# Attention and two MLPs in one kernel: the attention's pieces in a new order on TensorE, one ring for scores and transposes, and room of their own for three MLP operands

## Chip, cores and metric

One core of a Trainium2 chip. The metric is the device time of one execution in microseconds, the median of several runs. PE is TensorE, ACT ScalarE, DVE VectorE, POOL GpSimd, SP the engine that issues most DMAs.

## What is computed

Sigmoid attention over 4 batches, 12 heads, 448 positions of 64 values; its output, 1792 tokens of 768 values, goes through two MLPs of width 2048.

```python
scores = scale * np.matmul(q, k.transpose(0, 1, 3, 2)) - np.log(S)
attn = 1.0 / (1.0 + np.exp(-scores))
x = np.matmul(attn, v)                       # then (B*S, H*D)
h = x @ moe_w_in                             # first MLP: ELU
x = np.where(h > 0.0, h, np.exp(np.minimum(h, 0.0)) - 1.0) @ moe_w_out
h = x @ moe2_w_in                            # second MLP: h - tanh(h)
out = (h - np.tanh(h)) @ moe2_w_out
```

## The kernel before, in words

**Attention** runs over 24 pairs of heads (pair n is batch n // 6, heads 2(n % 6) and the next). Almost every product is made of three passes over a value's head and rest (the value rounded to fp32r, and what is left), so each operand needs a copy (the head, on ACT or DVE) and a subtraction (the rest, on DVE). For pair n:

- `t` (`transpose`, L302): four transposes of the queries (`t`, 0; 112-row pieces) and four of the keys (`t`, 1; 128-row pieces) on PE, into PSUM.
- `head` (L306, ACT) and `rest` (L311, DVE) bring them to SBUF as head and rest, in `e`, of which there are two, for even and odd pairs.
- `s` (`scores`, L336): for u = 0, 1, 2 six matmuls each, in which the two heads of the pair lie on the upper and lower 64 rows of the array (64x128 in the profile); for u = 3, the 64 positions left over of both heads together, three matmuls of 128x128.
- `sig` (L350, ACT): the sigmoid of one `s` piece. For u = 3 the result is split again: `ahead` (L359, ACT) and `arest` (L365, DVE).
- `pv` (L377, L384): for u = 0, 1, 2 two fp32 matmuls on 64 columns of the array each (128x64; four rows in the profile); for u = 3 three of 128x128. All four add into one PSUM bank.
- `xdone` (L395, ACT) copies that bank to `R0a`, `R0b`, `R1a` or `R1b`, the MLP's input (first or second half of the tokens; heads 0 to 5 or 6 to 11). POOL's `vhead` and `vrest` prepare the values for `pv`, 3.

PSUM during attention: three tiles of two banks for scores (`pss`, used in turn, (4n + u) % 3), one bank for transposes (`pst`), one for the output (`psv`).

**The order.** Each engine's instructions are written down by `Sched`: every operation has a queue, a cost, its predecessors and a rank. A greedy run over these costs starts, on each engine, what can start first, and of equal ones the lowest rank. `attention` chains its own operations: within one engine they stand strictly in the order of their rank, `when` = n x CYCLE + PHASES + SHIFTS (L70 to L84). PHASES says where in a pair's cycle a piece stands, and negative values put it into an earlier pair's. MLP operations carry ranks above 10^6 (but for the first weight loads, which have fixed ones) and fill in where the costs leave an engine free. On the chip each engine then works through its list in this order.

**The first MLP** begins right behind. It multiplies by Strassen-like schemes: the input of each half s of the tokens is turned into seven operands (B11, B21, T1, T2, B22, T3, T4; the T are differences), each with `x_sum` (L686, DVE), `x_head` (L692, ACT) and `x_rest` (L695, DVE), and the weights of each group into W0 to W3 (`w_head` L659, `w_rest` L662). Seven products P1, P2, P5, P6, P3, P7, P4 of nine matmuls each (`m_p`, L723) follow per group and half. P1, P2, P5 read B11, B21, T1 in tile `XA`, which exists from the start; P6, P3, P7, P4 read T2, B22, T3, T4 in `XB0`, which is opened (`open_late`) in the room that attention leaves, so its operands wait for the last `xdone` (`FIRST`, `before_late`). P3 and P7 read the weights W2, which are written over the inputs in `R0a` and `R0b` once all seven operands have been made from them. `snap` (L735) takes PSUM results out, `h_add` (L740), `g_a`, `g_b`, `g_c` finish them, `g_store` (L779, SP) stores them as `hidden`.

What is behind the opening (the rest of both MLPs, some 800 us) keeps its order on every engine.

Of the kernel before, what the change touches and what calls it, by code (L numbers as in the profile page):

```python
# [16 lines left out]
class Sched:  # L17
# [52 lines left out]
CYCLE = 8976  # L70
PHASES = {
    ("ahead", 0): 13136, ("ahead", 1): 14379, ("ahead", 2): 7982, ("ahead", 3): 8647,
    ("arest", 0): 13603, ("arest", 1): 17151, ("arest", 2): 17901, ("arest", 3): 18480,
    ("head", 0): -11764, ("head", 1): -8326, ("ldk",): -43986, ("ldv",): -25986, ("pv", 0): -2074,
    ("pv", 1): 1121, ("pv", 2): 3246, ("pv", 3): 4235, ("rest", 0): -564, ("rest", 1): 4498,
    ("s", 0): -12986, ("s", 1): -11085, ("s", 2): -11076, ("s", 3): -7628, ("sig", 0): 316,
    ("sig", 1): 2153, ("sig", 2): 3042, ("sig", 3): 3134, ("t", 0): -23560, ("t", 1): -17682,
    ("vhead",): 12413, ("vrest",): 13504, ("xdone",): 15024,
# [8 lines left out]
def kernel(  # L87
# [27 lines left out]
    ON_ACT = (2, 3)  # L115
    NAN, NAH, NAF, NVL, NL = 8, 3, 2, 2, 2
# [26 lines left out]
    XA = raw_p.tile([128, 3 * SLOT[0]], F32R, tag="XA", name="XA")  # L143
    raws = {(tag, 0): raw_p.tile([128, n], F32, tag=tag, name=tag) for tag, n in RAW.items()}
# [9 lines left out]
    with tc.manual_schedule():  # L154
# [7 lines left out]
        def attention():  # L162
# [178 lines left out]
            def width(u):  # L341
                return 2 if u < 3 else 1
# [1159 lines left out]
```

## Time and profile before

| | us |
|---|---|
| median of three runs | 1044.06 (1043.88 to 1046.54) |
| the profiled execution | 1043.71 |
| its span, first to last instruction | 1041.9 |
| PE busy in it | 1025.7 (98%) |
| PE weight loads | 877.8 (84%) |
| DVE busy | 635.3 (61%) |
| ACT busy | 579.1 (56%) |
| POOL busy | 93.2 (9%) |

The busy time of PE counts matmuls that overlap in the pipeline as one stretch, with modelled ends; it says that PE has work, not that it works at its densest. What a piece takes is read better from the start of its first matmul to the start of the next piece's. Attention lasts from the start to about 183 us; in each 20 us of it up to 180 us the mean granted clock is 1.00 (of 2.4 GHz).

### The profile page before, as it was taken

How to read it: one execution, taken by the hardware profiler on the slowest of the kernel's cores; microseconds unless marked ns; L12 is line 12 of the kernel's file. 1: busy time of each engine (PE TensorE's matmuls, PEld its weight loads, DVE VectorE, ACT ScalarE, POOL GpSimd, SP SyncE). 2: the span in 40 equal slices, each digit the busy share in tenths (PEclk: the TensorE clock that was granted, in tenths of full speed). 3: DMA queues.
4: the chain of work that ended last, by engine and by line, in shares of the span. 5: the costliest groups of instructions: out<-in, count | busy, mean ns of one | idle time of the engine just before them, and what ended most of it. 6: DMA issues, size and time to landing. Idle time of an engine off the chain costs nothing.

```text
span 1041.9 us, 15205 instructions
## 1 busy us (share of the span) xinstructions
PE 1025.7 (98%) x5420; PEld 877.8 (84%) x5420; DVE 635.3 (61%) x901; ACT 579.1 (56%) x930; POOL 93.2 (9%) x122
## 2 busy tenths in 40 slices
PE   8999999999999999999999999999999999999998
PEld 5555554779899998878899998889888999999998
DVE  2332354877676756665553459766666779665673
ACT  6777877866666665443332426433444546445652
POOL 1101110201221100000000202111111000000000
PEclk9999999999999999999999999999999999999999
DMA  7564430167766658999986300544444795455443
GB/s 171 156 165 122 95 75 23 36 208 239 257 227 222 225 169 289 345 324 368 357 297 207 104 1 21 212 154 154 155 154 154 266 320 198 133 170 172 130 136 92
DMA packets 151738, 190.26 MB, mean 183 GB/s; under 512 B 57072, under 2 KB 114672, under 8 KB 151408
## 3 DMA queue, kind: packets, MB, share of 16 engines
q1 hardware_dynamic: 150096, 188.72, 55.7%
q8 instruction: 42, 0.69, 0.3%
q10 hardware_dynamic: 1568, 0.59, 0.2%
q14 instruction: 32, 0.26, 0.1%
HBM read 125.30 MB, written 63.96 MB: 182 GB/s over the span
## 4 chain that ended last, share of the span: by engine, by line
PE 86%; DMA 5%; DVE 4%; ACT 2%; issue 1%; SPq 1%; ACTq 0%; DVEq 0%
PE psa L723 12%; PE psd L723 10%; PE psx L723 9%; PE sps L336 6%; PE pvps L377 6%; PE psb L723 5%; PE psa L869 3%; PE psx L869 3%; PE psb L869 3%; PE psw L869 3%; PE psv L869 3%; PE psu L869 3%; PE psd L925 3%; PE psx L925 3%; PE tps L302 2%; PE psb L925 2%
## 5 line engine op out<-in xcount | busy, mean ns | idle before, releaser
L311 DVE TENSOR_TENSOR e<-tps,e 128x448 fp32r<-128x448 f32 (+1 forms) x46 | 30.1, 654 | 91.2 <-ACT e L306 91.2
L336 PEld LDWEIGHTS sps<-e 64*128 64x128 f32 (+1 forms) x504 | 51.1, 185 | 25.7 <-ACT e L306 15.5
L336 PE MATMUL sps<-e 64*128 64x448 f32 (+1 forms) x504 | 71.3, 378 | 0.0
L377 PE MATMUL pvps<-an,vl 128*64 128x448 f32 x288 | 69.4, 563 | 0.6 <-ACT R1b L395 0.6
L350 ACT ACTIVATE an<-sps,bias 128x896 f32<-128x896 f32 x72 | 69.7, 1009 | 0.3 <-PE sps L336 0.3
L645 POOL TENSOR_TENSOR second<-second 128x384 f32<-128x384 f32 x15 | 18.0, 1199 | 509.3 <-DMA second<-kept_wi 370.1
L723 PE MATMUL psa<-XB,W 128*128 128x512 f32 x192 | 54.3, 391 | 0.4 <-ACT t L735 0.4
L850 ACT ACTIVATE XB<-t 128x384 fp32r<-128x384 f32 (+1 forms) x59 | 33.3, 566 | 18.2 <-PE psw L869 3.7
L723 PEld LDWEIGHTS psa<-XB,W 128*128 128x128 f32 x192 | 36.0, 188 | 8.4 <-ACT t L735 0.9
L645 POOL TENSOR_TENSOR first<-first,second 128x384 f32<-128x384 f32 x30 | 37.0, 1233 | 40.5 <-DVE R0b L662 39.3
L306 ACT ACTIVATE e<-tps 128x448 fp32r<-128x448 f32 (+1 forms) x46 | 26.2, 570 | 23.8 <-PE tps L302 21.3
L752 ACT ACTIVATE spare<-t 128x512 f32<-128x512 f32 (+1 forms) x30 | 17.5, 583 | 36.6 <-DVE t L740 34.1
L854 DVE TENSOR_TENSOR XB<-t,XB 128x384 fp32r<-128x384 f32 (+1 forms) x59 | 35.7, 614 | 3.3 <-ACT XB L850 3.3
L750 ACT ACTIVATE spare<-t 128x512 f32<-128x512 f32 (+1 forms) x39 | 22.4, 577 | 25.4 <-DVE t L740 23.8
L850 ACT ACTIVATE XB<-spare 128x384 fp32r<-128x384 f32 (+1 forms) x45 | 25.6, 569 | 19.4 <-DMA spare<-x_forms 9.3
L906 ACT ACTIVATE XB<-t 128x384 fp32r<-128x384 f32 (+1 forms) x36 | 20.1, 566 | 28.9 <-PE psb L925 15.1
L756 ACT ACTIVATE spare<-spare 128x384 f32<-128x384 f32 (+1 forms) x64 | 35.7, 572 | 0.7
L723 PE MATMUL psa<-XA,e 128*128 128x512 f32 x144 | 36.0, 394 | 0.0
L723 PE MATMUL psb<-XA,e 128*128 128x512 f32 x144 | 35.8, 393 | 0.0
L723 PE MATMUL psd<-XA,W 128*128 128x512 f32 x144 | 35.2, 389 | 0.0
L566 DVE TENSOR_SCALAR first<-first 128x768 int32<-128x768 int32 x32 | 17.9, 558 | 27.1 <-ACT first L563 26.8
L723 PE MATMUL psa<-XB,R0a 128*128 128x512 f32 x96 | 31.9, 416 | 2.2 <-ACT t L735 2.2
(400 smaller groups left out, 2751.1 us busy)
## 6 DMA issues: line engine op xcount, KB each, us to landing
R1b<-in_moe_w_out_dram SPq DMA_DIRECT2D x20, 768.0 KB, 5.8
first<-in_moe_w_in_dram SPq DMA_DIRECT2D x14, 768.0 KB, 6.3
second<-in_moe_w_in_dram SPq DMA_DIRECT2D x14, 768.0 KB, 6.6
x_forms<-R1b SPq DMA_DIRECT2D x29, 256.0 KB, 2.0
t<-x_forms SPq DMA_DIRECT2D x27, 256.0 KB, 3.2
hidden<-t SPq DMA_DIRECT2D x26, 256.0 KB, 2.0
R1a<-in_moe_w_out_dram SPq DMA_DIRECT2D x8, 768.0 KB, 7.7
t<-x_forms SPq DMA_DIRECT2D x32, 192.0 KB, 2.4
```

Source lines behind the costliest of these rows:

```text
L306: nc.scalar.activation(out=es[n % 2][:, slot, :W], in_=T["t", n, w][:, :W], func=ACTF.Copy)
L311: nc.vector.tensor_tensor(out=e[:, to, :W], in0=T.pop(("t", n, w))[:, :W], in1=f(e[:, slot, :W]), op=ALU.subtract)
L336: nc.tensor.matmul(out=ps[:, j, :S], lhsT=e[lanes, ks, cols], rhs=e[lanes, qs, :S], start=(x == 0), stop=(x == 2),)
L350: nc.scalar.activation(out=a[:, :m], in_=T.pop(("s", n, u))[:, :m, :S], func=ACTF.Sigmoid, bias=bias, scale=scale)
L377: nc.tensor.matmul(out=ps[D * j:D * j + D], lhsT=vl[n // NL % NVL][:, n % NL, 5 * j + u], rhs=a[:, j], start=(u == 0), stop=False,)
L645: by.tensor_tensor(out=out, in0=x, in1=y, op=op)
L723: nc.tensor.matmul(out=ps, lhsT=w[wz][:, k0:k0 + 128], rhs=xs[xz][:, kk], start=(opens and n == 0), stop=(n == 3 * KH - 1), skip_group_che ...
L756: nc.scalar.activation(out=r, in_=r, func=ACTF.Exp, scale=-1.0)
L850: nc.scalar.activation(out=at_place(og_place[s, p, j], 0, 1)[:, :HW[s]], in_=T["graw", s, p, j], func=ACTF.Copy)
L854: nc.vector.tensor_tensor(out=lo, in0=T.pop(("graw", s, p, j)), in1=f(hi), op=ALU.subtract)
L869: nc.tensor.matmul(out=T["o2", tag], lhsT=g[:, t * 128:t * 128 + 128], rhs=w[:, j % 2 * DH:(j % 2 + 1) * DH], start=(p in OPENS and j == 0 ...
L925: nc.tensor.matmul(out=ps, lhsT=lhsT, rhs=rhs, start=(opens and x == 0), stop=(ends_ and x == 2), skip_group_check=True,)
```

## The change

Attention's table of ranks is new (one cycle is 6900 instead of 8976 units, and almost all of SHIFTS goes). Its effect on the order is shown below. Besides:

- Scores and transposes share the ring of three two-bank tiles, five uses a pair, (5n + u) % 3; both transposes of a pair go into the two halves of one tile, written before its turn comes (`before_s` names what must have been read). The bank of their own goes.
- The output gets a second bank, used in turn: `pv`, 0 waits for `xdone` two pairs back, not one.
- `ahead` and `xdone` move from ACT to DVE.
- Fewer SBUF buffers for attention (`an` 8 to 6, `ah` 3 to 2); the room goes to `XB0`, now with T2, B22 and T3 alone and open from the start, so that these can be made as soon as their inputs are there. T4 goes to a small tile `XB2`, opened late as before. Places of later operands are renamed to match, in the same room.
- W1 and W3 and three PSUM banks, opened early, wait for `xdone` of the last pair but one too.

```diff
-CYCLE = 8976
+CYCLE = 6900
 PHASES = {
-    ("head", 0): -11764, ("head", 1): -8326, ("ldk",): -43986, ("ldv",): -25986, ("pv", 0): -2074,
...
+    ("s", 0): 0, ("s", 1): 620, ("s", 2): 1240, ("s", 3): 1900, ("pv", 3): CYCLE + 2500,
+    ("t", 1): 3100 - 2 * CYCLE, ("t", 0): 3500 - 2 * CYCLE, ("pv", 0): 4000, ("pv", 1): 4900, ("pv", 2): 5800,
...
+    ("ldk",): 4000 - 5 * CYCLE, ("ldv",): 3300 - 2 * CYCLE,
 }
...
-    ON_ACT = (2, 3)
-    NAN, NAH, NAF, NVL, NL = 8, 3, 2, 2, 2
+    NAN, NAH, NAF, NVL, NL = 6, 2, 2, 2, 2
...
+    XB0 = raw_p.tile([128, 3 * SLOT[0]], F32R, tag="XB0", name="XB0")
...
-            pst = apool("pst", 1, early, space=bass.MemoryType.PSUM, side="right")
...
-            psv = apool("psv", 1, space=bass.MemoryType.PSUM)
+            psv = [apool("psv0", 1, early, space=bass.MemoryType.PSUM, side="right")]
+            psv += [apool("psv1", 1, space=bass.MemoryType.PSUM)]
...
-                if (n, w) == (0, 1):
-                    ps = pss[0].tile([128, 2, BK], F32, tag="s", name="sps")[:, 0]
...
-                T["t", n, w] = ps
+                if ("tps", n) not in T:
+                    T["tps", n] = pss[(5 * n - 6) % 3].tile([128, 2, BK], F32, tag="s", name="sps")
+                T["t", n, w] = ps = T["tps", n][:, w]
...
-                T["s", n, u] = ps = pss[(4 * n + u) % 3].tile([128, 2, BK], F32, tag="s", name="sps")
+                T["s", n, u] = ps = pss[(5 * n + u) % 3].tile([128, 2, BK], F32, tag="s", name="sps")
...
-                if u in ON_ACT:
-                    nc.scalar.activation(out=t[:, 0], in_=a[:, 0], func=ACTF.Copy)
-                else:
-                    nc.vector.tensor_copy(out=t[:, 0], in_=a[:, 0])
+                nc.vector.tensor_copy(out=t[:, 0], in_=a[:, 0])
...
-                    T["o", n] = psv.tile([128, 512], F32, tag="o", name="pvps")[:, :S]
+                    T["o", n] = psv[n % 2].tile([128, 512], F32, tag="o", name="pvps")[:, :S]
...
+            def before_s(n, x):
+
+                n, x = divmod(5 * n + x - 3, 5)
+                return [("sig", n, x)] if x < 4 else [("rest", n + 2, 0), ("rest", n + 2, 1)]
...
-                op("xdone", n, (), "ACT", 700 if pairs[n][0] == 2 else 550, xdone, [("pv", n, 3)] + before)
+                op("xdone", n, (), "DVE", 700 if pairs[n][0] == 2 else 620, xdone, [("pv", n, 3)] + before)
...
-                    for n, s in enumerate(SLOT):
-                        tiles[f"XB{n}"] = pools["xb"].tile([128, 4 * s], F32R, tag=f"XB{n}", name=f"XB{n}")
+                    for name, n in (("XB1", 4 * SLOT[1]), ("XB2", SLOT[0])):
+                        tiles[name] = pools["xb"].tile([128, n], F32R, tag=name, name=name)
...
-                    name, at = ("XA", j) if j < 3 else ("XB0", j - 3)
+                    name, at = ("XA", "XB0", "XB2")[j // 3], j % 3
...
+            before_early += [("xdone", last - 1)]
...
-                     "XA": [], "XB0": before_late, "XB1": before_late, "R0a": [], "R0b": [], "R1a": [], "R1b": []}
+                     "XA": [], "XB0": [], "XB1": before_late, "XB2": before_late, "R0a": [], "R0b": [], "R1a": [], "R1b": []}
```

PE, one pair in the middle of attention, before (`sps` scores, `tps` transposes, `pvps` the output's bank; x18 are the scores of u = 0, 1, 2, x3 with `e` those of u = 3, x3 with `ah` is `pv`, 3):

```order
L336 MATMUL sps<-e_122 128x448 x18
L377 MATMUL pvps<-an,vl_119 64x448 x2
L302 MATMUL tps<-ident,first 128x128 x4
L377 MATMUL pvps<-an,vl_119 64x448 x2
L336 MATMUL sps<-e_122 128x448 x3
L377 MATMUL pvps<-an,vl_119 64x448 x2
L302 MATMUL tps<-ident,first 128x112 x4
L384 MATMUL pvps<-ah,vs_120 128x448 x3
```

and in the changed kernel (`sps` now holds scores and transposes):

```order
L333 MATMUL sps<-e_81 128x448 x21
L378 MATMUL pvps<-ah,vs_122 128x448 x3
L299 MATMUL sps<-ident,kq_118 128x128 x4
L299 MATMUL sps<-ident,kq_118 128x112 x4
L371 MATMUL pvps<-an,vl_119 64x448 x6
```

Eight pieces have become five: all scores together, the `pv`, 3 of the pair before, both transposes (of the pair after next), the other three `pv` together.

DVE, end of attention and start of the MLP, before (`XB_1909` is tile XB0, `XB_1910` XB1, `R0b<-second,R0a` the weights W2; the `e`, `W` rows are W0, W1, W3):

```order
L662 TENSOR_TENSOR e_80<-spare,e_80 128x768
L365 TENSOR_TENSOR ah<-a,ah 128x448
L662 TENSOR_TENSOR W_1868<-second,W_1868 128x768
L662 TENSOR_TENSOR W_1869<-spare,e_80 128x384
L695 TENSOR_TENSOR XB_1909<-R0b,XB_1909 128x1536
L695 TENSOR_TENSOR XB_1909<-R0a,XB_1909 128x1536 x2
L695 TENSOR_TENSOR XB_1909<-R0b,XB_1909 128x1536
L740 TENSOR_TENSOR t<-t,psb 128x512
L695 TENSOR_TENSOR XB_1910<-R1a,XB_1910 128x1152
L662 TENSOR_TENSOR R0b<-second,R0a 128x768
```

and in the changed kernel (`XB_1893` is XB2, `XB_1892` XB1; `COPY R1b` is `xdone`, `CAST` `ahead`):

```order
L653 TENSOR_TENSOR e_81<-spare,e_81 128x768
L389 COPY R1b<-pvps 128x448
L355 CAST ah<-a 128x448
L359 TENSOR_TENSOR ah<-a,ah 128x448
L653 TENSOR_TENSOR W_1851<-second,W_1851 128x768
L389 COPY R1b<-pvps 128x448
L653 TENSOR_TENSOR W_1852<-spare,e_81 128x384
L686 TENSOR_TENSOR XB_1893<-R0b,XB_1893 128x1536
L731 TENSOR_TENSOR t<-t,psb 128x512
L686 TENSOR_TENSOR XB_1892<-R1a,XB_1892 128x1152
L653 TENSOR_TENSOR R0b<-second,R0a 128x768
```

Three of the four rests of 1536 columns between W3 and W2 are gone from here; they stand among the rows of pairs 19 to 21 of the attention.

## Rows read from the trace of the kernel before

**Rows 1.** Timeline, PE alone, one whole pair: start us, us, engine, line, out<-in, shapes, count
```profile
41.89 2.09 PE L336 MATMUL sps<-e 64*128 64x448 f32 x18
43.91 0.97 PE L377 MATMUL pvps<-an,vl 128*64 128x448 f32 x4
44.81 0.66 PE L302 MATMUL tps<-ident,kq 128*128 128x128 f32 x4
45.40 0.97 PE L377 MATMUL pvps<-an,vl 128*64 128x448 f32 x4
46.30 0.87 PE L336 MATMUL sps<-e 128*128 128x448 f32 x3
47.10 0.97 PE L377 MATMUL pvps<-an,vl 128*64 128x448 f32 x4
48.01 0.60 PE L302 MATMUL tps<-ident,kq 112*128 112x112 f32 x4
48.38 0.85 PE L384 MATMUL pvps<-ah,vs 128*128 128x448 f32 x3
49.16 0.48 PE L336 MATMUL sps<-e 64*128 64x448 f32 x2
```

**Rows 2.** Timeline of the first pair's scores
```profile
9.56 2.89 PE L336 MATMUL sps<-e 64*128 64x448 f32 x21
10.48 2.81 ACT L350 ACTIVATE an<-sps,bias 128x896 f32<-128x896 f32 x3 [0.27 <-PE sps L336]
10.63 1.29 SPq L214 DMA_DIRECT2D kq<-in_k_dram  x2
11.58 0.50 PEld L336 LDWEIGHTS sps<-e 128*128 128x128 f32 x3 [0.30 <-ACT an L350]
12.29 0.55 PE L302 MATMUL tps<-ident,kq 112*128 112x112 f32 x4
```

**Rows 3.** The instructions on tile kq in the first 30 us, last line of the answer
```profile
DMA to landing us min/median/max: 2.4/2.9/3.4
```

**Rows 4.** Timeline, PE alone, end of the last pair
```profile
179.79 2.48 PE L377 MATMUL pvps<-an,vl 128*64 128x448 f32 x12 [0.63 <-ACT R1b L395]
182.20 0.88 PE L384 MATMUL pvps<-ah,vs 128*128 128x448 f32 x3
```

**Rows 5.** Groups by line and shape, 27 to 118 us: count | busy us, mean ns | idle before, releaser
```profile
L350 ACT ACTIVATE an<-sps,bias 128x896 f32<-128x896 f32 x37 | 35.9, 1007 | 0.0
L365 DVE TENSOR_TENSOR ah<-a,ah 128x448 fp32r<-128x448 f32 x13 | 8.0, 614 | 0.0
```

**Rows 6.** Busy time per stretch: length, PE, PEld, DVE, ACT, POOL, granted clock, DMA share, GB/s
```profile
41.90:49.20 7.30, 7.30 (x47) 3.97 (x46) 1.84 (x3) 6.03 (x9) 0.78 (x3) 1.00 0.58 173
196.00:198.20 2.20, 2.20 (x7) 1.71 (x6) 2.17 (x3) 2.19 (x4) 0.31 (x1) 0.50 0.41 159
```

**Rows 7.** Timeline, ACT and DVE: a sum, a head and a rest of MLP operands
```profile
122.37 1.97 DVE L686 TENSOR_TENSOR R0a<-R0a 128x1536 f32<-128x1536 f32 x1 [2.75 <-ACT R0a L395]
183.56 1.48 ACT L692 ACTIVATE XB<-R0b 128x1536 fp32r<-128x1536 f32 x1
185.07 1.76 DVE L695 TENSOR_TENSOR XB<-R0b,XB 128x1536 fp32r<-128x1536 f32 x1 [2.67 <-ACT XB L692]
```

**Rows 8.** Timeline, PE and ACT: the waits in the MLP's opening
```profile
189.69 2.33 PE L723 MATMUL psa<-XB,W 128*128 128x512 f32 x9 [0.45 <-ACT t L735]
194.62 0.50 PE L723 MATMUL psd<-XB,R0b 128*128 128x512 f32 x1 [1.92 <-DVE R0b L662]
226.35 1.16 PE L723 MATMUL psa<-XB,R0a 128*128 128x512 f32 x2 [2.16 <-ACT t L735]
225.70 0.60 ACT L735 ACTIVATE t<-psa 128x512 f32<-128x512 f32 x1 [3.45 <-DMA hidden<-t]
```

**Rows 9.** Chain of waits that ended last, in order of time: start us, us, what
```profile
197.06 3.11 PE psa L723 x9
249.55 2.04 PE psa L723 x9
```

More of the change, by code (lines that the diff above doesn't have):

```diff
@@ L402, in op @@
                 sch.op(key, queue, cost, lambda: fn(*args), after, when(kind, n, *rest), latency)
-            def back(kind, i, by):
-                return (kind, *divmod(i, by))
-            def before_t(n, w):
-                if (n, w) in ((0, 0), (0, 1), (1, 1)):
-                    return []
-                return [("rest", n, 0)] if w else [("rest", n - 1, int(n > 2))]
+            def before_s(n, x):
+                n, x = divmod(5 * n + x - 3, 5)
+                return [("sig", n, x)] if x < 4 else [("rest", n + 2, 0), ("rest", n + 2, 1)]
             for n in range(NPR):
@@ L418, in attention @@
                 for w in (1, 0):
-                    op("t", n, (w,), "PE", (390, 440)[w], transpose, loaded("qk"[w], n) + before_t(n, w))
-                    op("head", n, (w,), "ACT", (530, 600)[w], head, [("t", n, w)] + used)
-                    op("rest", n, (w,), "DVE", (610, 690)[w], rest, [("head", n, w)])
+                    op("t", n, (w,), "PE", (420, 440)[w], transpose, loaded("qk"[w], n) + before_s(n - 2, 4))
+                    op("head", n, (w,), "ACT", (550, 600)[w], head, [("t", n, w)] + used)
@@ L422, in attention @@
+                    op("rest", n, (w,), "DVE", (620, 690)[w], rest, [("head", n, w)])
                 op("vhead", n, (), "POOL", 800, vhead, loaded("v", n) + [("pv", n - 2, 3)])
-                op("vrest", n, (), "POOL", 1400, vrest, [("vhead", n)])
+                op("vrest", n, (), "POOL", 1200, vrest, [("vhead", n)])
                 for u in range(4):
-                    m2, i = width(u) == 2, 4 * n + u
-                    op("s", n, (u,), "PE", 610, scores,
-                       [("rest", n, 0), ("rest", n, 1), back("sig", i - 3, 4)])
-                    op("sig", n, (u,), "ACT", (550, 980)[m2], sig, [("s", n, u)] + ([back("pv", 3 * n + u - NAN, 3)] if m2 else [("arest", n - NAF, u)]))
+                    m2 = width(u) == 2
+                    op("s", n, (u,), "PE", 620, scores, [("rest", n, 0), ("rest", n, 1)] + before_s(n, u))
+                    was = ("pv", *divmod(3 * n + u - NAN, 3)) if m2 else ("arest", n - NAF, u)
+                    op("sig", n, (u,), "ACT", 1010 if m2 else 640, sig, [("s", n, u), was])
@@ L429, in attention @@
                     if not m2:
-                        op("ahead", n, (u,), *(("ACT", 500) if u in ON_ACT else ("DVE", 450)), ahead, [("sig", n, u), ("pv", n - NAH, u)])
-                        op("arest", n, (u,), "DVE", 620, arest, [("ahead", n, u)])
+                        op("ahead", n, (u,), "DVE", 450, ahead, [("sig", n, u), ("pv", n - NAH, u)])
+                        op("arest", n, (u,), "DVE", 650, arest, [("ahead", n, u)])
                 for u in range(4):
-                    op("pv", n, (u,), "PE", (630, 820)[width(u) - 1], pv,
-                       [("sig", n, u) if width(u) == 2 else ("arest", n, u)] + ([] if u else loaded("v", n) + [("xdone", n - 1)] + [("rest", 1, 1)] * (n == 0))
-                       + ([("vrest", n)] if u == 3 else []))
+                    op("pv", n, (u,), "PE", (620, 900)[width(u) - 1], pv,
+                       [("sig", n, u) if width(u) == 2 else ("arest", n, u)]
+                       + {0: loaded("v", n) + [("xdone", n - 2)], 3: [("vrest", n)]}.get(u, []))
@@ L459, in open_late @@
             def open_late():
-                if "XB0" not in tiles:
+                if "XB1" not in tiles:
                     open_early()
@@ L474, in flat @@
                     return e0.rearrange("p a t -> p (a t)")
-                if name in ("XB0", "XB1"):
+                if name == "XB0":
+                    return XB0
+                if name in ("XB1", "XB2"):
                     open_late()
@@ L966, in mlp @@
             before_early = [(kind, last) + w for kind, w in (("rest", (0,)), ("rest", (1,)))]
-            before_early += [("s", last, u) for u in range(4)] + [("sig", last, u) for u in range(4) if (4 * last + u) % 3 == 0]
+            before_early += [("s", last, u) for u in range(4)] + [("sig", last, u) for u in range(4) if (5 * last + u) % 3 == 0]
+            before_early += [("xdone", last - 1)]
             before_late = [("xdone", last)]
```

26 lines of the change are left out of this document (9 added, 17 removed).

## The prediction

> **What bounds the kernel now.** I read the engine shares first: TensorE (PE) is busy nearly all the time, no other engine comes near. So the questions are how densely PE works inside a stage, and where it stands still. For the first I took the timeline of one attention pair on PE alone [rows 1]. From the scores at 41.89 to the next pair's at 49.16 is 7.27 us with no idle row: PE has a next instruction all the time. The reader should see that equal work takes unequal time by what follows it. A `pv` piece followed by something else takes 0.90 (43.91 to 44.81); three in a row at the end of the last pair take 2.41 (179.79 to 182.20) [rows 4], against 2.70. Key transposes before a `pv` take 0.59 (44.81 to 45.40), query transposes before the full-height `pv 3` take 0.37 (48.01 to 48.38), with only an eighth less to stream. So leaving one kind of matmul for one of another shape costs about 0.1 to 0.2 us, and a pair does it seven times: only query transposes and `pv 3` share a shape (128 rows by 128 columns). For the second question I took PE's waits and the chain. Attention has hardly any; the opening of the MLP, straight after it, has two of about 2 us [rows 8].
>
> Beside PE, in this pair ACT works 6.03 us and DVE 1.84 of 7.3 [rows 6]: ACT has 1.3 to spare, DVE plenty.
>
> **Part 1, the pair's order.** The arithmetic stays. The order on PE becomes scores 0 to 3, last pair's `pv 3`, the transposes of the pair after next, `pv 0` to `pv 2`. Step by step:
> - Scores: 2.02 and 0.80 apart today, 2.82 [rows 1]. The first pair has them together: 9.56 to 12.29, 2.73 [rows 2].
> - `pv 3` takes 0.78 (48.38 to 49.16) and changes shape on leaving; before transposes it does not. I take the 0.20 off: 0.58.
> - Key transposes, then query transposes, 0.40 and 0.56: the same 0.96 as today, the one change of shape moving from the first to the second.
> - `pv 0` to 2 together: 2.41 [rows 4].
>
> Sum 6.68, so 0.60 less than 7.27. Bounds: with the gains that rows show directly and nothing from `pv 3`, 0.38; with 0.2 for each of four changes of shape that go, 0.80. I stay near the middle because two of its three parts are measured as they will stand. Of the 24 pairs 22 are whole; the two at the end have no transposes and gain half: 22 x 0.60 + 2 x 0.3 = 13.8 us.
>
> The Trainium skill, "TensorEngine Tiling (Array Packing)", Key Properties, says that changing the tiling mode, not merely the tile, drains TensorE. By that rule the count goes from seven drains to three, and at a mean of 0.18 the gain would be 0.72 a pair, two to three us more in all; the joined scores in this trace gave only 0.09, so I stay with 0.60.
>
> **Does the ring hold?** Scores and transposes use a ring of three tiles, five uses a pair. The tight place: scores 3 takes the tile of scores 0 and waits for its sigmoid. That begins 0.92 after the scores (9.56 to 10.48) and takes 1.007 [rows 2, 5], so ends at 1.93; PE comes to scores 3 at 2.02 (11.58), and there the row already names ACT. Margin 0.1. The others are wide: transposes need sigmoid 1, free at 2.8, PE there at 3.3; the next scores 2 need the second `rest`, DVE done at about 6.5 where PE comes at 8.0. ACT loses `xdone` and a copy, about 1.1, and is through by 5.2 of 6.68; DVE gains both at no more than 0.614 each, the row of its 448-column subtract [rows 5]: 1.84 becomes 3.1. Queued behind `xdone` on DVE, which waits for `pv 3`, are `ahead` and the two `rest`, needed by next pair's `pv 3` and scores 2; the second output bank lets `pv 0` go on. POOL's `vhead` still waits for an old `pv 3`. All that hides under PE, at nothing; if PE's cover fell below 5.2 it would be ACT that bounds.
>
> **Part 2, what the new order costs.**
> - First pair: PE now does both transposes of pair 2 before `pv 0` of pair 0, where it used to do scores of pair 1. They need keys whose second small load is issued at about 11.3 (half of 10.63 plus 1.29) [rows 2], on SP in the same place, and lands 2.4 to 3.4 later [rows 3]: 13.7 to 14.7. PE is there at 12.29. Wait 1.4 to 2.4; I take 1.9.
> - After each of the two idle times of about 2 us the granted clock fell: 0.50, the 1.2 GHz level, in 196.0 to 198.2 [rows 6]. From 194.62 to the end of the piece at 197.06, 200.17, 16 matmuls took 5.55; at 2.04 for nine they take 3.63 [rows 9]. So 1.9 is added. I charge it once for the new early wait; nought is the other bound.
> - `XB0` having its own room moves three heads and three rests of MLP operands into pairs 18 to 21, beside the sums and the three operands of `XA` that attention holds already and that now meet a shorter pair. A sum of 1.97 [rows 7] in front of DVE's `rest` makes the next scores 2 late by about 0.3, two of them by 1; two heads of 1.48 in a row delay a sigmoid by 0.4. Five such places, 2 us in all; nought to 4.
>
> 13.8 - 1.9 - 1.9 - 2.0 = 8.0 us.
>
> **Part 3, the opening.** Today four operands of the first half (T2, B22, T3, T4) can be written only after the last `xdone`: DVE does their rests of 1.76 [rows 7] one after the other, and the weights that PE wants for its fifth product stand behind them. PE waits 0.45 at 189.69 and 1.92 at 194.62 [rows 8], then has the low clock, 1.9: 4.3 us. Now only T4 is left there; DVE has three rests, 5.3, less in front of these weights. Four products of 2.04 [rows 9] bring PE to them at 8.2 after the first one starts; DVE, in its new order, does T4's rest, an addition that waits for the second product (4.1 plus some 0.9), one rest three quarters as large (1.3) and the weights' own, half as large (0.9): 7.2. I count all 4.3. What is late next: operands of the second half, also on DVE, earlier by the same 5 us as PE is; I subtract 0.4. Then a wait stays, 2.16 at 226.35, which comes from a store (ACT at 225.70 waits 3.45 for `hidden<-t`) [rows 8] behind weight loads. Loads, stores and products all move together, so I count no change.
>
> **Sum.** 8.0 + 4.3 - 0.4 = 12 us. The profiled execution took 1043.71; 1031.5. The median of the runs is 1044.06, 0.35 above it, no difference here.
>
> **The rivals.**
> 1. *The ring binds.* The 0.1 margin is used up, scores 3 waits in each pair, and of part 1 only the `pv` gain of 0.29 is left: 7.0 - 5.8 + 3.9 = 5, so 1038.5. For it: the row of scores 3 already waits for ACT. Against: that same row stands inside the 2.73. Chance 0.17.
> 2. *The store's wait goes too.* If the loads no longer stand in front of that store, 2.16 and the low clock after it go as well, 4.1: 1027.5. For it: DVE and ACT free the buffers earlier. Against: SP's order is the same. Chance 0.13.
> 3. *The clock falls in attention; slower.* With no margin on the ring, PE stops shortly in many pairs, and each drop adds up to 1.9 [rows 9]. Place: scores 3 and scores 2. Drops in seven pairs eat the whole gain; in every second pair they give 1031.5 + 23 = 1054. Against: PE stood 0.45 at 189.69 and the next rows show no slow stretch. The Trainium skill, "TensorE: Matmul & The Clock Gate", A second HAM failure mode: psum-queue depth-cycling, tells of just this, a kernel that cycles PSUM buffers and whose short idle times make the clock swing. By that rule rival 3 would be likelier; the trace of before, whose ring of three runs 24 pairs at full clock, speaks against it. Chance 0.08.
> 4. *No gain at all:* rival 1, and the opening's gain lost again at the store, 1042. The instruction order shows the pieces joined and the operands early, so the change does do what it says. Chance 0.05.
>
> My forecast has 0.55; 0.02 is for other outcomes.
>
> **Numbers.** Predicted 1031.5. The range takes rivals 1 and 2 and the bounds of part 1 (0.38 to 0.80 a pair is -5 to +5 us): 1022 to 1040, which leaves out rivals 3 and 4 and some of the edges. A measurement of this kernel can tell about 0.3%, 3 us. Faster by more: 0.55 + 0.17 + 0.13 + 0.02 = 0.87; same 0.05; slower 0.08.
>
> **What would show it.** Right: scores to scores about 6.7 us in the middle of attention with no idle row, `pv` as one group of 12 rows in 2.4; a wait of about 2 us near 12.3 on a key load; the last `pv 3` about 8 us earlier; no wait before the fifth product. Wrong: an idle row of scores on ACT in each pair (rival 1), granted clock under 1 between 30 and 120 us (rival 3), no wait some 43 us into the MLP (rival 2). If pairs still take 7.2 with PE never idle, my reading of the changes of shape is wrong.

## The result, and the profile after

The changed kernel takes 1028.43 us (median of 4 runs, 1027.59 to 1030.02), the kernel before, run beside it, 1045.21: ratio 0.9841, with a 95% interval of 0.982 to 0.9862. The forecast was 1031.5, its range 1022 to 1040. The profiled execution took 1027.59 (span 1025.8, before 1041.9), so the two traces differ by 16.1 us.

PE alone, one whole pair in the middle of attention (start us, us, engine, line, out<-in, shapes, count), to be read against [rows 1]:

```profile
65.72 2.91 PE L333 MATMUL sps<-e 64*128 64x448 f32 x21
68.46 0.78 PE L378 MATMUL pvps<-ah,vs 128*128 128x448 f32 x3
69.08 0.98 PE L299 MATMUL sps<-ident,kq 128*128 128x128 f32 x8
69.99 2.48 PE L371 MATMUL pvps<-an,vl 128*64 128x448 f32 x12
72.39 0.47 PE L333 MATMUL sps<-e 64*128 64x448 f32 x2
```

From one pair's scores to the next pair's are 6.67 us (65.72 to 72.39), where it was 7.27. The pieces, each from its start to the next one's, are: scores 2.74, `pv 3` 0.62, both transposes 0.91, `pv 0` to 2 together 2.40. The trace has 23 such distances; 17 of them are 6.67 to 6.69, and the first of the two pairs without transposes has 5.84.

Busy time by stretch (length; PE, PEld, DVE, ACT, POOL, each with its count; granted clock; DMA share; GB/s), the pair above, the first pair's scores, and the stretch after the store's wait:

```profile
65.72:72.39 6.67, 6.67 (x46) 4.34 (x44) 2.77 (x7) 5.18 (x7) 0.75 (x2) 1.00 0.92 240
10.00:16.00 6.00, 6.00 (x28) 4.53 (x27) 1.32 (x2) 3.96 (x5) 0.75 (x3) 0.50 0.87 195
213.00:215.00 2.00, 2.00 (x12) 1.76 (x11) 1.92 (x3) 1.61 (x3) 0.00 (x0) 1.00 0.84 324
```

The same for the kernel before, after its store's wait:

```profile
227.00:229.00 2.00, 2.00 (x6) 1.53 (x5) 1.53 (x3) 1.60 (x4) 0.00 (x0) 0.50 0.85 330
```

ACT and DVE work 5.18 and 2.77 us of a pair, so neither bounds it [rows 6]. The other rows matter below: in the changed kernel the clock was at its lower level in the first pair (0.50, which is 1.2 GHz), and at the upper one after the store's wait (1.00), where in the kernel before it was at the lower one.

The first pair in the timeline, against [rows 2]:

```profile
9.50 0.98 PE L299 MATMUL sps<-ident,first 112*128 112x112 f32 x4 [1.08 <-DMA first<-in_q_dram]
10.41 5.15 PE L333 MATMUL sps<-e 64*128 64x448 f32 x21
15.36 1.28 PE L299 MATMUL sps<-ident,kq 128*128 128x128 f32 x8
```

The scores take 4.95 us (10.41 to 15.36), where the kernel before took 2.73. The transposes of pair 2 follow at once, with no wait for their keys: what was late before PE came has landed while PE was slow.

PE's idle times after that, and the places that measure the stages (`psa<-XA,e` x9 is the first product of a group), against [rows 8]:

```profile
114.77 0.87 PE L333 MATMUL sps<-e 128*128 128x448 f32 x3 [0.22 <-ACT an L347]
...
148.84 1.68 PE L333 MATMUL sps<-e 64*128 64x448 f32 x9 [0.33 <-DVE e L308]
173.38 2.25 PE L714 MATMUL psa<-XA,e 128*128 128x512 f32 x9
187.64 0.72 PE L714 MATMUL psa<-XB,e 128*128 128x512 f32 x2 [0.22 <-DVE t L731]
197.79 2.25 PE L714 MATMUL psa<-XA,e 128*128 128x512 f32 x9
211.40 0.60 ACT L726 ACTIVATE t<-psa 128x512 f32<-128x512 f32 x1 [3.36 <-DMA hidden<-t]
212.05 0.73 PE L714 MATMUL psa<-XB,R0a 128*128 128x512 f32 x2 [2.03 <-ACT t L726]
```

Where the time came from:
- **Attention, with its start:** the first product starts at 173.38; before, at 182.92. That is 9.54.
- **Opening:** first product to first product of the next group is 24.41, before 29.00 (182.92 to 211.92). That is 4.59; the waits of 0.45 and 1.92 are gone, and so is the low clock behind them.
- **After the store's wait:** the wait is 2.03, before 2.16. From its end to the next `psx` product are 2.17 us (212.05 to 214.22), before 3.75 (226.35 to 230.10), for the same nine matmuls: the clock, 1.00 against 0.50. That is 1.6, and 1.7 with the shorter wait.

Together these are 15.8 of 16.1. The third part comes and goes in the runs below with one and the same order, so it is not put down to the change.

### The profile page after: what moved, and what is told of

It is laid out like the page before. It is cut to its first block, busy times and chain, and to the rows that moved or that the text cites. A ratio compares the mean times of both kernels' runs of the same rounds, so it can differ in the third digit from the quotient of the medians.

```text
span 1025.8 us, 15258 instructions
## 1 busy us (share of the span) xinstructions
PE 1011.9 (99%) x5420; PEld 886.9 (86%) x5420; DVE 655.9 (64%) x955; ACT 557.6 (54%) x876; POOL 94.0 (9%) x122
## 4 chain that ended last, share of the span: by engine, by line
PE 90%; DVE 3%; DMA 3%; ACT 2%; issue 1%; POOL 1%; SPq 0%; ACTq 0%; DVEq 0%; POOLq 0%
PE psa L714 11%; PE psd L714 9%; PE psx L714 9%; PE sps L333 6%; PE pvps L371 5%; PE psb L714 5%; PE psv L916 3%; PE psb L916 3%; PE psa L916 3%; PE psu L916 3%; PE psa L860 3%; PE psx L860 3%; PE psb L860 3%; PE psv L860 3%; PE psw L860 3%; PE psu L860 3%
## 5 line engine op out<-in xcount | busy, mean ns | idle before, releaser
L347 ACT ACTIVATE an<-sps,bias 128x896 f32<-128x896 f32 x72 | 67.6, 1006 | 39.9 <-PE sps L333 39.6
L371 PE MATMUL pvps<-an,vl 128*64 128x448 f32 x288 | 59.4, 548 | 0.0
L308 DVE TENSOR_TENSOR e<-sps,e 128x512 fp32r<-128x512 f32 (+1 forms) x48 | 31.3, 655 | 22.5 <-ACT e L303 20.9
L371 PEld LDWEIGHTS pvps<-an,vl 128*64 128x64 f32 x288 | 18.5, 136 | 26.0 <-issue 22.4
L845 DVE TENSOR_TENSOR XB<-t,XB 128x384 fp32r<-128x384 f32 (+1 forms) x59 | 35.8, 616 | 2.2 <-ACT XB L841 2.2
L901 DVE TENSOR_TENSOR XB<-t,XB 128x384 fp32r<-128x384 f32 (+1 forms) x36 | 21.9, 614 | 18.2 <-ACT XB L897 18.2
```

The lines of the kernel that those rows point to most:

```text
L308: nc.vector.tensor_tensor(out=e[:, to, :W], in0=T.pop(("t", n, w))[:, :W], in1=f(e[:, slot, :W]), op=ALU.subtract)
L347: nc.scalar.activation(out=a[:, :m], in_=T.pop(("s", n, u))[:, :m, :S], func=ACTF.Sigmoid, bias=bias, scale=scale)
L371: nc.tensor.matmul(out=ps[D * j:D * j + D], lhsT=vl[n // NL % NVL][:, n % NL, 5 * j + u], rhs=a[:, j], start=(u == 0), stop=False,)
L845: nc.vector.tensor_tensor(out=lo, in0=T.pop(("graw", s, p, j)), in1=f(hi), op=ALU.subtract)
```

## The experiments

The runs were made on four occasions, and the kernel before was run beside each; ratios are to that. The changed kernel's own is 0.9841.

**Old order, new resources.** Only the table of PE's order (and of ACT's and DVE's ranks with it) goes back; ring, banks, engines and room stay.

```diff
-    ("s", 0): 0, ("s", 1): 620, ("s", 2): 1240, ("s", 3): 1900, ("pv", 3): CYCLE + 2500,
-    ("t", 1): 3100 - 2 * CYCLE, ("t", 0): 3500 - 2 * CYCLE, ("pv", 0): 4000, ("pv", 1): 4900, ("pv", 2): 5800,
+    ("s", 0): 0, ("s", 1): 620, ("s", 2): 1240, ("pv", 0): CYCLE + 1900, ("t", 1): 2800 - 2 * CYCLE,
+    ("pv", 1): CYCLE + 3200, ("s", 3): 4100, ("pv", 2): CYCLE + 4700, ("t", 0): 5600 - 2 * CYCLE, ("pv", 3): CYCLE + 6000,
...
```

> The changed kernel with PE's old order of pieces in a pair (scores 0 to 2, pv 0, key transposes, pv 1, scores 3, pv 2, query transposes, pv 3 of the same pair), but with the new ring, the second output bank, the copies on DVE and the early XB0. Theory (a change of the matmul's shape costs 0.1 to 0.2 us, seven a pair instead of three): a pair takes 7.27 us again instead of 6.68, no idle rows on PE, so about 13 us more than the changed kernel's 1028.4: 1040 to 1043. Rival (the gain came from the resources, the ring, the bank or ACT's relief): pairs stay at 6.7 to 6.9, 1028 to 1033.

Measured: 1062.96 (1061.39 to 1064.98), ratio 1.0177 (1.0151 to 1.0202), slower than both kernels, which neither theory expected. PE alone, two neighbouring pairs, and the whole of attention by stretch:

```profile
66.58 2.53 PE L333 MATMUL sps<-e 64*128 64x448 f32 x18
73.58 0.60 PE L299 MATMUL sps<-ident,first 112*128 112x112 f32 x4 [0.37 <-ACT e L303]
74.73 1.50 PE L333 MATMUL sps<-e 64*128 64x448 f32 x12
76.76 0.87 PE L333 MATMUL sps<-e 64*128 64x448 f32 x6 [0.53 <-DVE e L308]
```

```profile
20.00:170.00 150.00, 138.52 (x801) 71.33 (x802) 63.84 (x109) 88.11 (x116) 18.18 (x36) 1.00 0.44 111
```

The pair is 8.15 us (66.58 to 74.73). Two waits are new: both transposes share one ring tile, so the query half, standing apart, waits 0.37 for ACT's head of the key half; and in every second pair or so scores 2 wait for the second `rest`, 0.53 here. So the ring fits the new order alone, and this run cannot price the order: something gentler was needed, below. It does bear on rival 3. PE stood idle in nearly every pair, 138.52 us busy of 150, and the granted clock was 1.00. The Trainium skill, "TensorE: Matmul & The Clock Gate", A second HAM failure mode: psum-queue depth-cycling, tells of a kernel in which short idle times between groups of matmuls made the clock swing; this trace shows nothing of it.

**Five changes of shape a pair instead of three.**

```diff
-    ("t", 1): 3100 - 2 * CYCLE, ("t", 0): 3500 - 2 * CYCLE, ("pv", 0): 4000, ("pv", 1): 4900, ("pv", 2): 5800,
+    ("pv", 0): 3100, ("t", 1): 3900 - 2 * CYCLE, ("t", 0): 4300 - 2 * CYCLE, ("pv", 1): 4900, ("pv", 2): 5800,
```

> The changed kernel with one difference: both transposes stand between pv 0 and pv 1 instead of ahead of pv 0. PE changes its shape of matmul five times a pair instead of three; ring, banks, engines and room are those of the changed kernel. Theory (each change of shape costs 0.1 to 0.2 us): pv 3 in front of pv 0 takes 0.78 where it takes 0.62 now, pv 0 in front of transposes 0.90 where it takes 0.80; with 2.73 for the scores, 0.96 for the transposes and 1.61 for the last two pv the pair is 6.98, 0.30 longer than 6.68, 22 times: +6.6 us, 1035 (1033 to 1037), and no idle row of PE in a middle pair. Rival (the gain came from the ring or from the moved room, not from the shapes): 1028 to 1029.

Measured: 1041.36 (1039.64 to 1043.56), ratio 0.9977 (0.9962 to 0.9992). Twice the loss expected: middle pairs take 7.23, not 6.98. The timeline of one pair's scores, with their weight loads (PEld) and DVE:

```profile
67.89 1.11 PEld L333 LDWEIGHTS sps<-e 64*128 64x128 f32 x12 [0.70 <-issue]
67.89 3.16 PE L333 MATMUL sps<-e 64*128 64x448 f32 x21
68.61 0.62 DVE L308 TENSOR_TENSOR e<-sps,e 128x448 fp32r<-128x448 f32 x1
69.34 0.53 PEld L333 LDWEIGHTS sps<-e 64*128 64x128 f32 x6 [0.34 <-issue]
```

The scores take 3.00 (67.89 to 70.89) instead of 2.74. The weight loads of scores 2 are due 1.11 after the first, at 69.0; they start at 69.34, just after the second `rest` has ended at 69.23. The row names no releaser, so it is only a reading that the `rest` has become late: it ends 1.34 after the scores have begun, where in the changed kernel, the row below, it ends 0.59 after (72.98 against 72.39). The next run tries it.

```profile
72.36 0.62 DVE L308 TENSOR_TENSOR e<-sps,e 128x448 fp32r<-128x448 f32 x1
```

**Five changes, the rest first.** The same, and on DVE the second `rest` goes ahead of `arest`:

```diff
-    ("ahead", 3): 4500, ("rest", 1): 5050 - 2 * CYCLE, ("arest", 3): 5100, ("rest", 0): 5700 - 2 * CYCLE,
+    ("ahead", 3): 4500, ("rest", 1): 5050 - 2 * CYCLE, ("arest", 3): 5800, ("rest", 0): 5700 - 2 * CYCLE,
```

> The run with five changes of shape once more, with the wait that disturbed it taken out: there the second rest ended at 69.23, after PE had come to scores 2, because DVE did the subtract of pv 3's weights (arest, 0.61) in front of it. Here the rest goes first and arest behind it. Theory (shapes cost 0.1 to 0.2 each, the rest of that run's loss was the ring): the scores take 2.73 to 2.75 again instead of 2.99, the pair 2.74 + 0.71 + 0.90 + 0.97 + 1.66 = 6.98, 0.30 longer than the changed kernel's 6.68; 22 times: 1034 to 1036. Rival (order costs the whole 0.55 by itself): pairs stay at 7.23 and the time at 1041.

Measured: 1034.09 (1033.69 to 1034.87), ratio 0.992 (0.9901 to 0.9938). PE alone, one pair:

```profile
66.42 2.91 PE L333 MATMUL sps<-e 64*128 64x448 f32 x21
69.17 0.77 PE L378 MATMUL pvps<-ah,vs 128*128 128x448 f32 x3
69.87 0.97 PE L371 MATMUL pvps<-an,vl 128*64 128x448 f32 x4
70.78 1.04 PE L299 MATMUL sps<-ident,kq 128*128 128x128 f32 x8
71.75 1.72 PE L371 MATMUL pvps<-an,vl 128*64 128x448 f32 x8
73.41 2.91 PE L333 MATMUL sps<-e 64*128 64x448 f32 x21
```

The pair takes 6.99 us with no idle row, piece for piece as added up: two more changes of shape cost 0.31. The work, the ring and the engines are the same; only the neighbours differ. That shape counts, and not just a change of operands, is seen on `pv 3`: in front of the transposes, which share its shape, it takes 0.62 in the changed kernel, in front of `pv 0` 0.70 here.

**Control: the rest first, order of the changed kernel.** Only this of the edits above:

```diff
-    ("arest", 3): 5100,
+    ("arest", 3): 5800,
```

> Control for the run with five changes and the rest first: the changed kernel with only arest behind the second rest on DVE, PE's order unchanged. Theory: the ring has slack in the middle pairs, so they stay at 6.68 and only the one wait of scores 2 on DVE's rest beside the MLP's operands (0.33 at 148.84) can go: 1027.5 to 1029. Rival (the rest binds in the middle pairs too): pairs under 6.65 and 1024 or less. Other side: pv 3 waits for the later arest, an idle row on DVE ah in front of pv 3: 1031 or more.

Measured: 1026.39 (1023.72 to 1028.98), ratio 0.9845 (0.9819 to 0.9871): the changed kernel's. Middle pairs take 6.67 to 6.69. So the `rest` did not bind in the changed kernel's middle pairs, and the 0.31 above is the order's own.

**Seven changes.** As with five, but key transposes, `pv 1` and query transposes alternate, so that a pair has as many changes as in the kernel before.

```diff
-    ("t", 1): 3100 - 2 * CYCLE, ("t", 0): 3500 - 2 * CYCLE, ("pv", 0): 4000, ("pv", 1): 4900, ("pv", 2): 5800,
+    ("pv", 0): 3100, ("t", 1): 3900 - 2 * CYCLE, ("pv", 1): 4300, ("t", 0): 5200 - 2 * CYCLE, ("pv", 2): 5800,
```

> As the run with five, but pv 0, key transposes, pv 1, query transposes, pv 2: seven changes of shape a pair, as many as in the kernel before, in the changed kernel's ring. Theory: 2.73 + 0.78 + 0.90 + 0.59 + 0.90 + 0.56 + 0.81 = 7.27 a pair, 0.59 longer than 6.68, 22 times: +13 us, 1041.5 (1039 to 1044), without a wait for the ring; the pieces have the durations that they have in the kernel before. Rival (the shapes are not it): 1028 to 1029. Middle case: the second rest comes later by 0.8 than in the changed kernel, and if scores 2 wait for it, an idle row shows there and the time is above 1044.

Measured: 1054.11 (1052.42 to 1058.61), ratio 1.0107 (1.008 to 1.0134). This is the middle case, and worse than it had it: most pairs take 7.9 to 8.5 us, because the query transposes wait 0.57 for work on the key half of their tile, or scores 2 wait 0.2 to 0.9 for the second `rest`. Five pairs, between them, have no wait; one of these, PE alone:

```profile
57.84 2.92 PE L333 MATMUL sps<-e 64*128 64x448 f32 x21
60.59 0.78 PE L378 MATMUL pvps<-ah,vs 128*128 128x448 f32 x3
61.30 0.97 PE L371 MATMUL pvps<-an,vl 128*64 128x448 f32 x4
...
64.22 0.97 PE L371 MATMUL pvps<-an,vl 128*64 128x448 f32 x4
65.12 1.10 PE L333 MATMUL sps<-e 64*128 64x448 f32 x8
```

It takes 7.28 us, the 7.27 of [rows 1] in another sequence. So 3, 5 and 7 changes give 6.67, 6.99 and 7.28, on the mean 0.15 us for each. The Trainium skill, "TensorEngine Tiling (Array Packing)", Key Properties, has a change of tiling mode drain TensorE; these rows agree in that each change costs time, and give its price, but they do not show what TensorE does in it.

**One output bank.**

```diff
-                    T["o", n] = psv[n % 2].tile([128, 512], F32, tag="o", name="pvps")[:, :S]
+                    T["o", n] = psv[1].tile([128, 512], F32, tag="o", name="pvps")[:, :S]
...
-                       + {0: loaded("v", n) + [("xdone", n - 2)], 3: [("vrest", n)]}.get(u, []))
+                       + {0: loaded("v", n) + [("xdone", n - 1)], 3: [("vrest", n)]}.get(u, []))
```

> The changed kernel with one output bank for pv instead of two: pv 0 of a pair now waits until xdone of the pair before has emptied the bank. Theory (the second bank is not what gives the gain): xdone takes 0.55 to 0.61 on DVE after pv 3, and PE does both transposes, 0.96, in between, so the wait is hidden or under 0.1 us a pair: 1028 to 1031. Rival (the second bank is needed): DVE comes to xdone late behind another instruction, pv 0 waits 0.3 us or more in each of 23 pairs with a row on DVE: 1035 or more.

Measured: 1031.86 (1030.58 to 1032.49), ratio 0.9878 (0.9864 to 0.9893). PE alone, two of the five rows where `pv 0` waits:

```profile
143.81 2.48 PE L371 MATMUL pvps<-an,vl 128*64 128x448 f32 x12 [0.33 <-DVE R1a L389]
151.41 2.48 PE L371 MATMUL pvps<-an,vl 128*64 128x448 f32 x12 [0.67 <-DVE R1a L389]
```

The time is just above the theory's range. Middle pairs stay at 6.67 to 6.70: the transposes hide `xdone`. Late in attention, where DVE has MLP operands to write, five pairs wait, 2.9 us in all. So the second bank is worth about 3 us, and only beside the MLP's preparation.

**`ahead` and `xdone` on ACT again.**

```diff
-                nc.vector.tensor_copy(out=t[:, 0], in_=a[:, 0])
+                nc.scalar.activation(out=t[:, 0], in_=a[:, 0], func=ACTF.Copy)
...
-                op("xdone", n, (), "DVE", 700 if pairs[n][0] == 2 else 620, xdone, [("pv", n, 3)] + before)
+                op("xdone", n, (), "ACT", 700 if pairs[n][0] == 2 else 550, xdone, [("pv", n, 3)] + before)
```

> The changed kernel with the two copies ahead and xdone on ACT again. Theory (PE bounds the pair, ACT has room: 4.9 plus 1.1 of 6.68): quiet pairs stay at 6.68 to 6.75; pairs with a narrow or operand copies of MLP on ACT, about ten, lose up to 1 us each: 1029 to 1036. Rival (the move to DVE was needed for each pair): pairs at 7 or more, 1037 and up.

Measured: 1028.1 (1026.54 to 1030.52), ratio 0.9844 (0.9817 to 0.9871), the changed kernel's, and a little under the theory's range. The same 6.67 us by stretch:

```profile
65.72:72.39 6.67, 6.67 (x45) 4.34 (x46) 3.37 (x5) 6.05 (x10) 0.74 (x2) 1.00 0.68 165
```

In such a pair ACT works 6.05 of 6.67 and still holds nobody up. Beside the MLP's preparation PE waits 0.63 and 0.33 on ACT and 0.53 on DVE's `ah`, 1.5 us in all, where the changed kernel waits 1.1. This part of the change moved no time that these runs can tell.

**`XB0` late again.**

```diff
-                     "XA": [], "XB0": [], "XB1": before_late, "XB2": before_late, "R0a": [], "R0b": [], "R1a": [], "R1b": []}
+                     "XA": [], "XB0": before_late, "XB1": before_late, "XB2": before_late, "R0a": [], "R0b": [], "R1a": [], "R1b": []}
```

> The changed kernel, but XB0's operands wait for the last xdone as before. Theory: the opening of the MLP gets back the waits before the fourth and fifth product and the low clock after them, 4 to 4.6 us; attention loses the stalls that these operands cause in pairs 19 and 20, about 0.6 to 1 us: 1031 to 1033. Rival (the waits of the opening came from attention's late end, not from the operands): 1027 to 1029. If the wait on the store 39 us into the MLP is again followed by the low clock, 2 us more.

Measured: 1030.13 (1030.0 to 1032.79), ratio 0.987 (0.9841 to 0.9898). PE alone, the opening:

```profile
170.49 2.22 PE L714 MATMUL psa<-XA,e 128*128 128x512 f32 x9
179.27 0.73 PE L714 MATMUL psd<-XB,R0a 128*128 128x512 f32 x2 [0.43 <-ACT R0a L650]
181.25 0.50 PE L714 MATMUL psd<-XB,R0b 128*128 128x512 f32 x1 [1.25 <-DVE R0b L653]
187.74 0.72 PE L714 MATMUL psa<-XB,e 128*128 128x512 f32 x2 [0.98 <-DVE t L731]
...
198.76 2.34 PE L714 MATMUL psa<-XA,e 128*128 128x512 f32 x9
```

The waits are back, and the opening takes 28.27 where the changed kernel has 24.41: the room is worth 3.9 there. It costs 0.9 beside attention: from the second pair's scores to the first product are 153.54 us here (16.95 to 170.49) and 154.41 there (18.97 to 173.38). The clock stayed at 1.00 through this opening, so the 3.9 has no clock in it; the forecast 4 to 4.6 had. The time lies between the two ranges, and the difference from the changed kernel, 1.7 us, is within what these intervals leave open; the stage shows it, the total does not. The two traces differ at the start as well: in this execution the clock stayed up in the first pair, and the second pair's scores begin 2.0 us earlier, long before `XB0` is used.

**PE kept busy at the start.** Ten transposes without use are put into each of the two idle times before the first scores.

```diff
+                    for x, at in ((1, 3900 - 2 * CYCLE), (2, 3300 - CYCLE)):
+                        sch.op(("warm", x), "PE", 100, lambda: keep_warm(10), [], at)
```

> The changed kernel with twice ten transposes of the identity more on PE, in the two idle times before the first scores. They feed nothing. Theory (the low clock from 9.5 to 16 us comes from PE standing idle twice before): granted clock 1.00 there, the first scores take 2.73 instead of 5.0, but the wait for the key load of pair 2 (lands at about 14.4) now shows, about 1.2: gain 1 us, 1026.5 to 1028. Rival (the low clock there does not depend on these idle times): clock still 0.5, time within 0.3 of the changed kernel's or up to 0.5 more.

Measured: 1029.16 (1027.87 to 1030.95), ratio 0.9853 (0.983 to 0.9877). PE alone in the first pair, then two stretches:

```profile
12.71 1.68 PE L333 MATMUL sps<-e 64*128 64x448 f32 x9 [0.76 <-DVE e L308]
14.23 0.98 PE L299 MATMUL sps<-ident,kq 128*128 128x128 f32 x8
```

```profile
8.00:16.00 8.00, 7.24 (x59) 5.69 (x59) 2.93 (x5) 5.67 (x10) 1.44 (x4) 1.00 0.91 209
210.00:215.00 5.00, 4.10 (x13) 3.50 (x14) 3.10 (x5) 3.69 (x6) 0.00 (x0) 0.72 0.65 248
```

At full clock the first pair shows what the low clock had covered: scores 2 of pair 0 wait 0.76 for the `rest` of pair 1, through the ring. The expected wait for a key load does not come. The second pair's scores begin at 17.55, 1.4 us earlier than in the changed kernel. It was not worth anything in the end: here the clock fell after the store's wait instead, and the time is the same. That the added transposes kept the clock up is not shown: nine of the other eleven runs, without them, have 1.00 from 10 to 16 us as well.

**The store ahead of the loads.** Two weight loads of 768 KB wait, in the order, for a later instruction, so that a store of `hidden` goes first.

```diff
-    j0, j1 = (job(("wi", i, GC * g + c), False, p) for c, p in enumerate(places))
+    j0, j1 = (job(("wi", i, GC * g + c), False, p, [("g_c", (0, 0, 1), 0, 1)] if (i, g) == (0, 2) else []) for c, p in enumerate(places))
```

> The changed kernel with one difference in the MLP's second group: two weight loads of 768 KB on SP are issued behind the store of hidden, 192 KB, that stood behind them. Theory (the wait of 2.03 at 212.05 comes from that store, which lands 7.7 us after its issue because the loads go first): the store lands some 3 us after its issue, about 207, before the product that needs its buffer ends at 208.04; the wait goes, and with it the low clock that follows it in some executions: 1024.5 to 1026.5. Rival (the loads were needed in time): the weights of the third group come later and the wait appears there instead: 1028 to 1030.

Measured: 1031.85 (1031.06 to 1032.28), ratio 0.9879 (0.9864 to 0.9894). The DMA issued at 202 (count, KB, us to landing), and PE's waits after it:

```profile
hidden<-t SPq DMA_DIRECT2D x1, 192.0 KB, 2.8
```

```profile
219.85 0.62 PE L714 MATMUL psd<-R0a 128*128 128x384 f32 x2 [1.00 <-ACT t L726]
226.54 0.62 PE L714 MATMUL psx<-R1a,e 128*128 128x384 f32 x2 [1.19 <-DVE t L731]
```

The store lands in 2.8 us and its wait is gone, as the theory had it; 1.00, 1.19 and, at 278.41, 2.71 us of other waits take its place. The rival was right that the wait only moves, and the time is even above its range; but the longest of the new waits is on a later store (ACT waits 2.90 for `hidden<-t` before it), not on the weights.

**That store on ACT's queue.**

```diff
-                nc.sync.dma_start(
+                (nc.scalar if (step, c, b) == ((0, 0, 1), 1, 1) else nc.sync).dma_start(
```

> The changed kernel with one DMA moved: the store of hidden (192 KB) that stands on SP behind two weight loads is issued by ACT, on its own queue, at the same point in time; all else keeps its place. Theory (the wait of 2.03 at 212.05 is this store standing behind the loads in one queue): it lands 2 to 4 us after its issue instead of 7.7, the copy of the product's bank does not wait for its buffer, the wait goes, and 1.5 to 4 us of the time: 1024.5 to 1027. Rival A (not the queue but the bandwidth, which the loads use up): it lands 6 us or more after its issue, the wait stays: 1028 to 1029. Rival B (as when the loads were moved behind it): the wait goes and a later wait for a buffer takes its place: 1028 to 1029.

Measured: 1026.97 (1024.92 to 1027.03), ratio 0.9844 (0.9821 to 0.9868). The timeline where the wait was:

```profile
208.50 0.60 ACT L726 ACTIVATE t<-psa 128x512 f32<-128x512 f32 x1 [2.78 <-DMA hidden<-t]
209.15 0.73 PE L714 MATMUL psa<-XB,R0a 128*128 128x512 f32 x2 [1.34 <-ACT t L726]
```

Issued at 201.3, it lands 7.1 us later from a queue of its own, where it took 7.7 on SP's: by the landing this is rival A. The DMA engines are busy all the time there (share 1.02 in 205 to 210). The wait is 0.7 shorter, 1.34 for 2.03. The time lies in the theory's range, but the ratio is the changed kernel's, so it tells nothing between the two.

**A version meant to beat both.** The control, and the early fetch of the late weights begins one group later, so that 2.3 MB around the store become 1.5.

```diff
-                per = len(todo) / (NG - 1)
+                per = len(todo) / (NG - 2)
...
-                    ahead(todo.pop(0), 2, i, [("h", (i, g, 0), "P1")], True)
+                    ahead(todo.pop(0), 2, i, [("h", (i, g, 0), "P1" if g > 1 else "P3")], True)
```

> A version meant to beat both: the run with only the rest first, and beside it the early fetch of the late weights begins one group later, so that no 768 KB load of them and no store of theirs shares the transfers with the store of hidden at 203. If the wait of 2.0 to 2.4 at that store is a matter of bandwidth (moving the store to another queue took only 0.7 off it), its 192 KB then stand behind 1.5 MB instead of 2.3 MB, it lands before its buffer is wanted, and the wait goes, with the low clock that follows it in some executions: 1022 to 1025. Rival (as when the two loads were moved): another wait for a buffer or for the weights of a later group takes its place: 1026 to 1028.

Measured: 1027.55 (1026.79 to 1029.24), ratio 0.9864 (0.9842 to 0.9886): no better than the changed kernel. DMA issued from 199 to 204, then PE:

```profile
hidden<-t SPq DMA_DIRECT2D x2, 192.0 KB, 6.9
```

```profile
209.09 0.73 PE L714 MATMUL psa<-XB,R0a 128*128 128x512 f32 x2 [1.73 <-ACT t L726]
```

The two stores of these 5 us still take 6.9 and the wait is 1.73, so taking the third load away is not enough. Beside it a wait of 1.67 has come at 248.70, on a later store (ACT waits 2.19 for `hidden<-t`), and the time is the rival's. None of the versions tried beats the changed kernel by more than a measurement can tell.

## Why the prediction was right, and where it was not

The forecast was the likeliest case, and it came: faster, in the range, 3 us under the figure. (Its own terms add up to 11.9 us and so to 1031.8; 1031.5 is what was written down.) By its steps:

- **Part 1, the pair: right, and shown.** 6.68 forecast, 6.67 measured, and the pieces within 0.05. That it is the changes of shape, and not the ring, is shown by the pairs without a wait that have 5 and 7 changes in the changed kernel's own ring. For the whole of attention 13.8 was forecast. From the first scores to the first product are 162.97 us, before 173.36: 10.4 less. Adding what the low clock cost in the first pair (8.56 to the next scores where 6.06, a pair without a `pv 3`, was due: 2.5) and the pairs beside the MLP's preparation (1.8) gives 14.7; 0.63 of it is a wait at the end of the kernel before [rows 4] that is gone.
- **The ring holds.** Rival 1 did not come: no idle row in a middle pair. Its margins were mis-sized in one place. The second `rest` was given 1.5 us to spare; it ends at 72.98 where the weight loads of scores 2 are due at 73.50 (1.11 after 72.39), so it has 0.5. In the run with five changes it comes 0.75 later against the scores, and they wait. The ring is not what gives the gain: under the old order it loses 0.9 us a pair.
- **Part 2, the first pair: right in size, wrong in kind.** The forecast had a wait of 1.9 for keys, then 1.9 of low clock. The trace has no such wait. The clock had fallen already, after two waits of 1.1 for the first loads, and the first scores at half speed covered the keys: 3.3 us (0.85 later, and 2.5), against 3.8. Where the clock stays up, the wait for the keys is 0.2 to 0.3 (runs with one bank and with the store ahead) or does not show (control), and one of 0.4 to 0.8 stands before it, for the `rest` of pair 1 through the ring, which the forecast had not seen. So this step failed in its mechanism, and was right in sum by chance. The price of 1.9 for a fall was a little high as well: it counts the end of the last matmul. From 194.62 to the start of the next product, 199.99, the 16 matmuls take 5.37, which is 1.7 more than 3.63.
- **Part 2, the MLP's preparation: right.** Five places and 2.0 us were forecast; four pairs are longer, by 0.27, 0.45, 0.45 and 0.59, 1.8 together.
- **Part 3, the opening: right.** 4.3 less 0.4 was forecast, 4.59 measured, and undoing the room alone costs 3.9 of it. Of what was to be late next, only a wait of 0.22 came (187.64).
- **Part 3, the store's wait: it stays, as forecast, but the low clock after it was left out.** 2.16 became 2.03. Only the clock after it differs, 1.6 us, and nothing ties that to the change: with the same order and operand room it fell in the runs with PE kept busy and with `ahead` on ACT (0.72 and 0.71 in 210 to 215), and stayed up in the control, after a wait of 2.35. Rival 2 named the right place for the rest of the gain and the wrong cause: its wait did not go.
- **Rival 3** has no run for it: from 20 to 170 us the clock was 1.00 in the changed kernel (the row below), and in the run with the old order in the new ring, where PE is idle in nearly every pair, too.

```profile
20.00:170.00 150.00, 148.93 (x978) 96.42 (x974) 85.69 (x138) 109.02 (x144) 18.48 (x44) 1.00 0.47 117
```

Between the two traces 16.1 us are gained, where 11.9 were added up. Of the 4.2 more the opening has 0.7, the attention's sum 0.85 (0.63 of it that last wait), the early start 0.45, the preparation 0.25 and the store's wait with the clock after it 1.7; the rest lies in stages that were not followed. The clock differs from one execution of a kernel to another: its mean over the four of the changed kernel was 0.995 to 1.000. So single profiles of one and the same kernel may differ by such a fall.

## What to carry to other kernels

Where PE is never idle and still slow, count how often neighbouring matmuls differ in shape, and compare one piece's duration by what follows it: here each change took 0.15 us on the mean, and joining like with like gave 0.6 of 7.3. A ring of buffers shared by several users is tied to one order; before such an order is changed, write down for each use when its tile comes free and when PE wants it, and let the tightest consumer (here the second `rest`) go first on its engine. A gain at one stage is best checked at that stage, from one mark to the next: 3.9 us of room in the opening are plain there and lost in the total's interval.

## What the runs showed of the hardware that was not expected

- The granted clock does not follow from the length of one idle time alone. PE stood about 1 us twice before the first scores, in the changed kernel (1.06 and 1.08) and in the run with one bank (0.96 and 1.07): the clock was 0.50 afterwards in the one, 1.00 in the other. At the store it fell behind waits of 1.91 (`ahead` on ACT) and 2.28 (PE kept busy) and not behind 2.03 (changed kernel) and 2.35 (control). What decides it stays open.
- A fall of the clock can cost less than the slow stretch suggests: the first pair took 8.56 us at the lower level and 7.53 at the upper one, in the run with one bank, where waits of 0.77 and 0.18 stand that the slow scores had covered.
- A store of 192 KB took 2.8 us to land in front of two loads of 768 KB, and behind them 7.7 from the same queue and 7.1 from another.
